# Sliding-window attention mixed with a SwiGLU FFN: the softmax division in the tail, first sums in fp32, operands on multiples of 256 bytes, the first tail tile halved early

## The chip, the cores and the metric

The kernel runs on one core of a Trainium2 chip. The metric is the device time of one execution in microseconds (us), taken as the median of several executions. PE is TensorE (matmuls; PEld its weight loads), DVE is VectorE, ACT is ScalarE, POOL is GpSimd; SP issues nearly all DMAs and POOL the others.

## The reference

With x of 2048 x 512, 32 heads of 16, a causal window of W = 256 keys and an FFN of 1792 columns, all float32:

```python
scores = jnp.einsum("bhqd,bhkd->bhqk", q, k) * (Dh ** -0.5)
mask = (idx[:, None] - idx[None, :] >= 0) & (idx[:, None] - idx[None, :] < W)
p = _softmax(jnp.where(mask[None, None], scores, -1e9), axis=-1)
a = (p @ v, heads joined) @ wo                    # in short
b = (_silu(x @ w_gate) * (x @ w_up)) @ w_down
g = _sigmoid((x * gate_w).sum(-1, keepdims=True))
return g * a + (1 - g) * b
```

## The kernel before, in words

**Number format.** TensorE takes fp32r operands. To keep float32 precision, each operand is split into hi (a cast to fp32r) and lo (the rest), and every product is three matmuls: hi by hi, hi by lo, lo by hi. `split` makes the two; `mm3` issues the three. A cast runs on ACT or DVE, the subtraction on DVE or POOL. The program is a manual schedule: each engine runs its instructions in the order in which the code issues them, and waits by semaphores.

**Start (0 to 87 us).** Twelve-odd DMAs bring x (transposed, `xT`), the q/k weights and `wv`. `split_x` makes `xhi`/`xlo`, four chunks of 512 positions, that stay for the whole program. Eleven small products of `ident` warm TensorE. `proj(g, c)` makes q and k of group g (four heads) for chunk c, by `whole`: a PSUM bank of 128x512 and 12 matmuls. `vproj` makes v. `stack` copies the parts of q and k by DMA into `QT` and `KT`, 63 rows deep, so that one matmul gives a score with all three partial products; row 63 holds the maximum of the row (`QT`) and ones (`KT`). `stage1` makes scores of a block of 128 queries, and DVE adds the mask and takes the row's maximum; `put_max` transposes the maxima on PE by `ident`, negates them and loads row 63. `prefetch` fetches the next tile of FFN or q/k weights and `prepare` splits it on ACT (hi) and POOL (lo).

**Slots (87 to 611 us).** 129 slots, 16 for each of 8 groups. A slot has `stage1` of the next group, `stage2` of this one (transposed scores, exponent on ACT, masks on POOL), and a quarter of a unit of `lanes`: two 512-column sums at once, each product done as two matmuls of 64 rows that run beside each other. The units are the q/k sums of later groups and 26 of the 28 sums of the FFN's gate and up tiles; these go to DRAM (`raws`). Every fourth slot `av` multiplies probabilities by v (`vg`, with a column of ones that gives the softmax's sum), and `finish` adds the two half sums, transposes on DVE, takes the reciprocal, multiplies, transposes back and writes to `od` by a DMA of POOL. In the last group the gate is made (`gate_fetch`, `gate_block`), and eight tiles of w_down are split (`wd_early`).

**Tail (611 to 842 us).** 4 chunks c of 14 FFN tiles n. `hidden` loads the two sums of a tile (`got`), takes silu on ACT and the product on DVE; `halved` splits that into `hh` (ACT) and `hl` (DVE); `step(c, n)` is 12 matmuls that add this tile's part of the output for four blocks into four PSUM banks. Tile 13's sums are the two that the slots don't make: 24 matmuls in `hidden` itself. `ORDER` sets that tile as the second. `load_wd`, `load_wo` bring weights in chunk 0. `load_oc` loads attention's output from `od`, `attn_split` splits it (ACT, POOL), `attn_out` multiplies by wo. `put` adds the terms and writes the output. SP issues the loads in the code's order and each waits for its buffer, so a load behind a waiting one waits too.

Of the kernel before, what the change touches and what calls it, by code (L numbers as in the profile page):

```python
# [16 lines left out]
P = 128  # L17
# [16 lines left out]
def gated_mix(ctx, tc, xT, xn, wqk, wv, wo, wgu, wd, gw, out):  # L34
# [22 lines left out]
    gate = const.tile([P, NB], F32, name="gate")  # L57
    igate = const.tile([P, NB], F32, name="igate")
# [82 lines left out]
    ORDER = [0, NF - 1, *range(1, NF - 1)]  # L141
# [25 lines left out]
    with ExitStack() as A:  # L167
# [4 lines left out]
        for _ in range(11):  # L172
            nc.tensor.matmul(warm[:, :P], ident, ident, start=True, stop=True)

        mask = sm.tile([P, 3 * P], F32, name="mask", bufs=1)
        nc.gpsimd.memset(mask, 0.0)
        nc.gpsimd.affine_select(out=mask, in_=mask, pattern=[[-1, 3 * P]], compare_op=ALU.is_ge,
                                fill=NEG, base=W, channel_multiplier=1)
        nc.gpsimd.affine_select(out=mask, in_=mask, pattern=[[1, 3 * P]], compare_op=ALU.is_ge,
                                fill=NEG, base=-1, channel_multiplier=-1)  # L180
# [52 lines left out]
        def proj(g, c, pool, name):  # L233
# [9 lines left out]
            return whole(pool, name, products(("p", g), c), done)  # L243
# [10 lines left out]

# [21 lines left out]
        def put_max(g, hf):  # L276
            n = NB // 2
            mt = sm.tile([4 * n, P], F32R, name="mt")
            for o in HALVES:
                pt = ps1.tile([P, CH], F32, name="ps1")  # L280
                nc.tensor.matmul(pt[:4 * n, :64], MX[g, hf].rearrange("p h b -> p (h b)")[o], ident[o, o],
                                 start=True, stop=True)
                nc.vector.tensor_scalar(mt[:, o], pt[:4 * n, :64], -1.0, None, op0=ALU.mult)  # L283
            for pr in range(2):
                nc.sync.dma_start(halves_of(QT[g % 2][pr])[hf][63::64].bitcast(F32),
                                  mt[2 * pr * n:2 * (pr + 1) * n].bitcast(F32))
# [48 lines left out]
        def finish(g, c):  # L335


# [6 lines left out]
            if lo:  # L344
                nc.vector.tensor_copy(both[:, :lo], first[:, :lo])
            yield
            ot = osb.tile([P, CH], F32, name="ot")
            nc.vector.transpose(ot, both)
            yield
            v = ot.rearrange("p (s e) -> p s e", e=32)  # L350
            rc = osb.tile([P, CH // 32], F32, name="rc")
            nc.vector.reciprocal(rc, v[:, :, DH])
            nc.vector.tensor_tensor(out=v[:, :, :DH], in0=v[:, :, :DH],
                                    in1=rc[:, :, None].to_broadcast([P, CH // 32, DH]), op=ALU.mult)
            yield
            on = osb.tile([P, CH], F32, name="on")
            nc.vector.transpose(on, ot)
            nc.gpsimd.dma_start(od[g, :, c * CH:(c + 1) * CH], on)
# [8 lines left out]
        split_wq = weights(("p", 0))  # L367
# [14 lines left out]
        def v_products(b):  # L382
            c, o = divmod(b * P, CH)
            return [(xt[c][:, k, o:o + P], wt[:, k]) for k in range(NK)
                    for xt, wt in ((xhi, wvh), (xhi, wvl), (xlo, wvh))]
# [20 lines left out]
        xraw = [halves_of(h) for h in xraw]  # L406

        def split_x(c):
            for k in range(NK):
                split(xhi[c][:, k], xlo[c][:, k], xraw[2 * c + k // 2][k % 2], nc.scalar, nc.vector)  # L410

        for c in range(NCH):
            for k in range(NK):
                nc.sync.dma_start(xraw[2 * c + k // 2][k % 2], xT[c][:, k])
            if c == 0:
                split_next = weights(("p", 1), kept(), nc.vector)
                wvraw = [fetch(wv[:, k], kept()) for k in range(NK)]
        split_wq()
# [328 lines left out]
```

## Time and profile before

| what | value |
|---|---|
| runs | 842.01, 842.23, 843.0 us; median 842.23 |
| the profiled execution, its span | 842.1 us, granted TensorE clock 0.996 on average |
| PE busy | 826.0 us, 98% |
| DVE, ACT, POOL busy | 520.7, 448.4, 351.6 us |
| moved by DMA | 133.02 MB, mean 158 GB/s |
| waits of PE that the profile names | 3.9 us on hh at the tail's start, 2.6 on ACT's copy in `finish`, 1.5 on ACT's copy of v, 1.4 on `ident`, each other 0.6 or less |

The span runs from the first instruction to the last. A row of the profile reads: line, engine, operation, written tile <- read tiles, shape, count, then busy time and mean; in a timeline the start and the length come first, and brackets hold the idle time ahead and what ended it. PE's matmuls overlap (each is shown some 390 ns long and the next starts some 230 ns later), so their pace is read from start to start.

### The profile page before, as it was taken

What the parts mean: (1) busy time and instruction counts of PE and PEld (TensorE: products, weight loads), DVE (VectorE), ACT (ScalarE), POOL (GpSimd) and SP (SyncE); (2) the same over time, 40 slices, a digit from 0 to 9 for tenths busy, and PEclk for the clock granted to TensorE, in tenths of its full rate; (3) what the DMA queues carried; (4) which work ended last, traced back from release to release, by engine and by line L of the source; (5) the groups of instructions that cost most, each with busy time, mean ns of one, the idle gap of its engine ahead of it and who ended that gap; (6) DMA issues with size and microseconds to landing.
All of it is one profiled execution on the core that took longest, in us unless ns stands there. A gap on an engine that the chain in (4) does not pass through costs nothing. (4 is left out here: it accounts for less than half of the span.)

```text
span 842.1 us, 21678 instructions
## 1 busy us (share of the span) xinstructions
PE 826.0 (98%) x8390; PEld 709.7 (84%) x8390; DVE 520.7 (62%) x1438; ACT 448.4 (53%) x933; POOL 351.6 (42%) x638
## 2 busy tenths in 40 slices
PE   8999999999999999999999999999979999999998
PEld 6787899899888888988888889889858888888886
DVE  6396577667767676676677677655567353353443
ACT  5412666666656666666656666566545433243251
POOL 7702455546546555545554654456501121011020
PEclk9999999999999999999999999999989999999999
DMA  7574525624533543542552463466679544293451
GB/s 274 160 210 146 148 80 150 193 93 135 153 135 120 158 152 110 161 156 99 153 178 95 125 186 128 134 198 211 209 250 295 172 162 163 76 298 89 150 163 51
DMA packets 66007, 133.02 MB, mean 158 GB/s; under 512 B 9456, under 2 KB 14192, under 8 KB 65904
## 3 DMA queue, kind: packets, MB, share of 16 engines
q1 hardware_dynamic: 61936, 117.74, 44.7%
q0 software_dynamic: 3968, 13.90, 4.5%
q8 instruction: 66, 1.08, 0.5%
q14 instruction: 37, 0.30, 0.1%
HBM read 60.82 MB, written 45.35 MB: 126 GB/s over the span
## 5 line engine op out<-in xcount | busy, mean ns | idle before, releaser
L269 DVE CUSTOM_DVE_ANT_0 ps<-ps,mask 128x384 f32<-128x384 f32 (+2 forms) x512 | 272.1, 540 | 143.4 <-PE ps L267 67.1
L308 ACT ACTIVATE pt<-ps 128x384 f32<-128x384 f32 (+2 forms) x512 | 241.6, 478 | 117.2 <-PE ps L267 60.2
L310 POOL TENSOR_SCALAR_AFFINE_SELECT pt<-pt 128x256 f32<-128x256 f32 x256 | 108.3, 423 | 229.2 <-ACT pt L308 225.4
L306 PE MATMUL ps<-q,k 64*128 64x384 f32 (+2 forms) x512 | 163.8, 329 | 2.6 <-ACT on L341 2.6
L267 PE MATMUL ps<-k,q 63*128 63x384 f32 (+2 forms) x512 | 163.7, 329 | 0.3 <-DVE mt L283 0.3
L218 PE MATMUL pb<-xhi,wh 64*128 64x512 f32 x512 | 118.2, 393 | 0.0
L218 PE MATMUL pa<-xhi,wh 64*128 64x512 f32 x512 | 117.1, 395 | 0.1
L218 PE MATMUL pb<-xlo,wh 64*128 64x512 f32 x512 | 117.2, 390 | 0.0
L218 PE MATMUL pb<-xhi,wl 64*128 64x512 f32 x512 | 117.1, 389 | 0.0
L218 PE MATMUL pa<-xhi,wl 64*128 64x512 f32 x512 | 115.0, 391 | 0.0
L218 PE MATMUL pa<-xlo,wh 64*128 64x512 f32 x512 | 114.7, 390 | 0.0
L267 PEld LDWEIGHTS ps<-k,q 63*128 63x128 f32 x512 | 92.8, 184 | 11.2 <-issue 5.4
L306 PEld LDWEIGHTS ps<-q,k 64*128 64x128 f32 x512 | 93.6, 184 | 9.5 <-ACT on L341 4.4
L313 POOL TENSOR_SCALAR_AFFINE_SELECT pt<-pt 128x256 f32<-128x256 f32 x224 | 97.8, 437 | 0.0
L654 DVE TENSOR_TENSOR sg<-got,sg 128x512 f32<-128x512 f32 x52 | 44.0, 846 | 64.5 <-ACT sg L653 54.6
L330 PE MATMUL ps<-pt,vg 64*32 64x320 f32 (+4 forms) x1408 | 76.0, 346 | 0.0
L330 PE MATMUL pb<-pt,vg 64*32 64x320 f32 (+3 forms) x1360 | 74.9, 350 | 0.0
L269 DVE DVE_READ_ACCUMULATOR2_ANT mx<- 128x1 f32 x512 | 71.8, 140 | 0.0
L218 PEld LDWEIGHTS pb<-xhi,wh 64*128 64x128 f32 x512 | 64.2, 185 | 4.0
L218 PEld LDWEIGHTS pb<-xhi,wl 64*128 64x128 f32 x512 | 64.4, 184 | 3.4
L330 PEld LDWEIGHTS pb<-pt,vg 64*32 64x32 f32 x1360 | 48.9, 106 | 21.1 <-ACT pt L308 5.1
L218 PEld LDWEIGHTS pa<-xhi,wl 64*128 64x128 f32 x512 | 62.0, 184 | 4.7
(143 smaller groups left out, 1661.7 us busy)
## 6 DMA issues: line engine op xcount, KB each, us to landing
raws<-ev SPq DMA_DIRECT2D x104, 256.0 KB
got<-raws SPq DMA_DIRECT2D x104, 256.0 KB
od<-on POOLq DMA_DIRECT2D x32, 256.0 KB, 2.4
q<-xhi SPq DMA_DIRECT2D x56, 128.0 KB
k<-xhi SPq DMA_DIRECT2D x56, 128.0 KB
raw<-wgu SPq DMA_DIRECT2D x28, 256.0 KB
vd<-vs POOLq DMA_DIRECT2D x8, 672.0 KB, 5.0
vg<-vd SPq DMA_DIRECT2D x32, 168.0 KB
```

The costliest lines, as they stand in the source:

```text
L218: mm = nc.tensor.matmul(ps[me], w[r], x[r], start=not second and i == 0, stop=bool(second) and i == n - 1)
L267: nc.tensor.matmul(ps[:, :n], QT[g % 2][pr][r, q0:q0 + P], KT[g % 2][pr][r, k0:k0 + n], start=True, stop=True)
L269: mx = nc.vector.tensor_tensor_reduce(out=ps[:, :n], in0=ps[:, :n], in1=mask[:, 3 * P - n:], scale=1.0, scalar=NEG, op0=ALU.add, op1=ALU.m ...
L306: nc.tensor.matmul(ps[:, :n], KT[g % 2][pr][r, k0:k0 + P], QT[g % 2][pr][r, k0:k0 + n], start=True, stop=True)
L308: BEHIND.append(nc.scalar.activation(pt[:, j, :n], ps[:, :n], AF.Exp, scale=SCALE))
L310: nc.gpsimd.affine_select(out=pt[:, :, :P], in_=pt[:, :, :P], pattern=[[0, 2], [1, P]], compare_op=ALU.is_ge, fill=0.0, base=0, channel_mu ...
L313: nc.gpsimd.affine_select(out=pt[:, :, 2 * P:], in_=pt[:, :, 2 * P:], pattern=[[0, 2], [-1, P]], compare_op=ALU.is_ge, fill=0.0, base=-1, ...
L330: nc.tensor.matmul(AV[g, c][h][32 * j:32 * j + 32, q0 - c * CH:q1 - c * CH], VG[4 * g + kb // 4][o, kb % 4, 17 * j:17 * j + 32], PT[g, kb, ...
L654: nc.vector.tensor_tensor(out=sg, in0=gu[1], in1=sg, op=ALU.mult)
```

## The change

- Softmax's division leaves `finish`. The slots write undivided sums to `od`; in the tail `load_sums` loads the softmax sums, `invert` takes one reciprocal of 128x512 on DVE and writes it to `rd`; `load_oc` loads a piece of `od` and a broadcast piece of `rd`, POOL multiplies and writes the result back into place by a DMA of its own.
- The first q/k sums (chunk 0 of groups 0 and 1) are made from raw x and raw weights in float32, 4 products each in place of 12; the splits of these weights, the mask and the fills come behind. The warm-up is 6 products.
- `put_max` transposes on DVE and goes by DRAM (`mxd`); `get_max` loads row 63 a slot later; `KT`'s row 63 is -1.
- `gate` and `igate` (64 bytes a partition each) are allocated ahead of `xhi`/`xlo`.
- In the start, `prefetch` is issued ahead of the stacks, and banks pa and pb change roles in `vproj2` and the last `proj`.
- Tile 0 of chunk 0 is made and halved in slots 113 to 120 (silu by exp, add, reciprocal, two products); tile 13 is third in `ORDER`; six w_down tiles are early, eight in the tail; the gate is made four slots earlier.
- The last two steps are interleaved by block, each followed by its `put`.

```diff
+    gate = const.tile([P, NB], F32, name="gate")
+    igate = const.tile([P, NB], F32, name="igate")
     xhi, xlo = [], []
...
-    ORDER = [0, NF - 1, *range(1, NF - 1)]
+    MADE = 2
+    ORDER = [0, 1, NF - 1, *range(2, NF - 1)]
...
-        for _ in range(11):
+        for _ in range(6):
             nc.tensor.matmul(warm[:, :P], ident, ident, start=True, stop=True)
...
         def put_max(g, hf):
-            n = NB // 2
-            mt = sm.tile([4 * n, P], F32R, name="mt")
-            for o in HALVES:
-                pt = ps1.tile([P, CH], F32, name="ps1")
-                nc.tensor.matmul(pt[:4 * n, :64], MX[g, hf].rearrange("p h b -> p (h b)")[o], ident[o, o],
-                                 start=True, stop=True)
-                nc.vector.tensor_scalar(mt[:, o], pt[:4 * n, :64], -1.0, None, op0=ALU.mult)
+            mt = sm.tile([P, 32], F32, name="mt")
+            nc.vector.transpose(mt, MX[g, hf].rearrange("p h b -> p (h b)"))
+            u = 2 * g + hf
+            nc.sync.dma_start(mxd[u], mt)
...
         def finish(g, c):
...
-            ot = osb.tile([P, CH], F32, name="ot")
-            nc.vector.transpose(ot, both)
...
-            nc.vector.reciprocal(rc, v[:, :, DH])
...
-            nc.vector.transpose(on, ot)
-            nc.gpsimd.dma_start(od[g, :, c * CH:(c + 1) * CH], on)
+            nc.gpsimd.dma_start(od[g, :, c * CH:(c + 1) * CH], both)
...
+        def first_sums(g, w):
+            run(proj(g, 0, pp, "pa", [(w[:, k], xraw[0][k]) for k in range(NK)]))
...
         split_x(0)
-        split_next()
+        first_sums(0, wq0)
         for k in range(NK):
-            split(wvh[:, k], wvl[:, k], wvraw[k], *(dve if k % 2 else act))
-        for g in range(2):
-            run(proj(g, 0, pp, "pa"))
+            split(wvh[:, k], wvl[:, k], wvraw[k], nc.scalar, nc.gpsimd if k % 2 else nc.vector)
+        first_sums(1, wq1)
+        fill_rows(KT[0], -1.0, 0, nc.gpsimd)
+        make_mask()
+        split_w(0, wq0, nc.gpsimd)
+        split_w(1, wq1, nc.vector)
+        prefetch()
         split_x(1)
...
-            (a0, a1), (b0, b1) = vproj2(b, pp, "pa"), vproj2(b + 2, pp, "pb")
+            (a0, a1), (b0, b1) = vproj2(b, pp, "pb"), vproj2(b + 2, pp, "pa")
...
-        prefetch()
...
+        def first_tile():
+            e = kept()
+            nc.scalar.activation(e, g0, AF.Exp, scale=-1.0)
+            yield
+            nc.vector.tensor_scalar(e, e, 1.0, None, op0=ALU.add)
+            yield
+            nc.vector.reciprocal(e, e)
+            yield
+            nc.gpsimd.tensor_tensor(out=e, in0=g0, in1=e, op=ALU.mult)
...
+            split(hh0, hl0, e, nc.scalar, nc.vector)
...
+        def load_sums():
+            l = rp.tile([P, CH], F32, name="raw2")
+            nc.sync.dma_start(l, od.rearrange("g (j e) (q s) -> (g j) e q s", e=32, q=NCH)[:, DH])
+            return l
+
+        def invert(l):
+            nc.vector.reciprocal(l, l)
+            nc.sync.dma_start(rd.rearrange("h (q s) -> (h q) s", q=NCH), l)
...
         def load_oc(c, k):
...
-            nc.sync.dma_start(OC[c][:, k], heads[:, :DH, c * CH:(c + 1) * CH])
+            s = slice(c * CH, (c + 1) * CH)
+            nc.sync.dma_start(OC[c][:, k], heads[:, :DH, s])
+            nc.sync.dma_start(RC[c][:, k], rd[8 * k:8 * k + 8, None, s].to_broadcast([8, DH, CH]))
+
+            def divide():
+                o = bp.tile([P, CH], F32, name="o")
+                nc.gpsimd.tensor_tensor(out=o, in0=OC[c][:, k], in1=RC[c][:, k], op=ALU.mult)
+                nc.gpsimd.dma_start(OC[c][:, k], o)
+            return divide
...
+        def last_steps(two):
+            for b in range(4):
+                for t in two:
+                    block(b, *t)
+                put(two[0][0], b, ACC[two[0][0]][b], igate)
+
+        seq = [(c, n) for c in range(NCH) for n in range(NF)][1:]
+        loads = [(c, ORDER[n]) for c, n in seq if n != MADE]
...
+        fresh, waiting, ready = [], [(0, 0, hh0, hl0)], []
+        sums = load_sums()
         for c, n in seq:
...
-            if c == 0 and n < NF - 8:
-                ready.append(load_wd(ORDER[n + 8], pieces[n + 8], raw2()))
+            if c == 0 and n == 1:
+                ready.append(lambda: invert(sums))
+            if c == 0 and n + 5 < NF:
+                ready.append(load_wd(ORDER[n + 5], pieces[n + 5], raw2()))
...
             if c == 0 and n >= NF - 4:
-                load_oc(0, n - NF + 4)
-            if c and 1 <= n < 5:
-                load_oc(c, n - 1)
+                ready.append(load_oc(0, n - NF + 4))
+            if c and MADE < n < MADE + 5:
+                ready.append(load_oc(c, n - MADE - 1))
```

Three places show how the order changes. On SP in the start, where the first FFN weights (`raw<-wgu`) stand among the transfers of `stack` (`q<-x..`, `k<-x..`). Before:

```order
L251 DMA k_351<-x10lo 32x1024
L250 DMA q_349<-x10lo 32x1024
L251 DMA k_351<-x10hi 32x1024
L72 DMA raw<-wgu 128x512 x2
L285 DMA q_85<-mt 2x8x128
L285 DMA q_86<-mt 2x8x128
```

After:

```order
L416 DMA q_126<-xT 128x512 x4
L416 DMA k_127<-xT 128x512 x4
L416 DMA k_128<-xT 128x512 x4
L74 DMA raw<-wgu 128x512
L248 DMA q_87<-xhi 32x1024
L249 DMA k_89<-xhi 32x1024
```

The first weight load stood behind all 36 of the stacks' transfers and now stands ahead of the first of them.

On DVE at the tail's start: `sg` is silu times up, `hl` the low half of it, `q` and `k` the places of the w_down tiles, `raw` a buffer of 128x512 and `pb` the bank of tile 13. Before:

```order
L654 TENSOR_TENSOR sg<-got_10745,sg 128x512
L67 TENSOR_TENSOR hl<-sg,hh 128x512
L654 TENSOR_TENSOR sg<-pb,sg 128x512
L66 CAST q_348<-raw_10755 128x512
L67 TENSOR_TENSOR q_348<-raw_10755,q_348 128x512
L654 TENSOR_TENSOR sg<-got_10749,sg 128x512
L66 CAST q_348<-raw_10768 128x512
L67 TENSOR_TENSOR q_348<-raw_10768,q_348 128x512
L67 TENSOR_TENSOR hl<-sg,hh 128x512
```

After:

```order
L715 TENSOR_TENSOR sg<-got_10475,sg 128x512
L69 TENSOR_TENSOR hl<-sg,hh 128x512
L715 TENSOR_TENSOR sg<-pb,sg 128x512
L650 RECIPROCAL raw_10485<-raw_10485 128x512
L68 CAST q_331<-raw_10487 128x512
L69 TENSOR_TENSOR q_331<-raw_10487,q_331 128x512
L715 TENSOR_TENSOR sg<-got_10479,sg 128x512
L68 CAST q_331<-raw_10516 128x512
L69 TENSOR_TENSOR q_331<-raw_10516,q_331 128x512
L69 TENSOR_TENSOR hl<-sg,hh 128x512
```

The rows are those of tile 0 before and of tile 1 after, as the first tile; the reciprocal of the sums stands between tile 13's product and its `hl`, the last row.

On POOL in the tail: `wol` and `ol` are low halves of wo and of attention's output, `o` the divided output. Before, these five rows are all from the last of wo on:

```order
L67 TENSOR_TENSOR wol<-raw_11067,woh 128x512
L67 TENSOR_TENSOR ol<-xhi_69,oh 128x512 x4
L67 TENSOR_TENSOR ol<-xlo_70,oh 128x512 x4
L67 TENSOR_TENSOR ol<-xhi_71,oh 128x512 x4
L67 TENSOR_TENSOR ol<-xlo_72,oh 128x512 x4
```

After, from chunk 1's `ol` on (chunk 2's head follows):

```order
L69 TENSOR_TENSOR ol<-xlo_74,oh 128x512 x4
L662 TENSOR_TENSOR o<-xhi_75,xlo_76 128x512
L663 DMA xhi_75<-o 128x512
L662 TENSOR_TENSOR o<-xhi_75,xlo_76 128x512
L663 DMA xhi_75<-o 128x512
L662 TENSOR_TENSOR o<-xhi_75,xlo_76 128x512
L663 DMA xhi_75<-o 128x512
L662 TENSOR_TENSOR o<-xhi_75,xlo_76 128x512
L663 DMA xhi_75<-o 128x512
L69 TENSOR_TENSOR ol<-xhi_75,oh 128x512 x4
```

Between one chunk's `ol` and the next's stand four products and four DMAs of POOL's own, each behind its product.

More of the change, by code (lines that the diff above doesn't have):

```diff
@@ L384, in v_products @@
             return [(xt[c][:, k, o:o + P], wt[:, k]) for k in range(NK)
-                    for xt, wt in ((xhi, wvh), (xhi, wvl), (xlo, wvh))]
+                    for xt, wt in ((xhi, wvh), (xlo, wvh))] + \
+                   [(xhi[c][:, k, o:o + P], wvl[:, k]) for k in range(NK)]
         def put_v(b, ps):
@@ L527, in wd_early, with first_load, gate_done @@
             later(t, 2, lambda: later(t + 1, 2, load_wd(f, piece, kept())))
-        pieces = [h for two in (QT[0], KT[0], QT[1], KT[1]) for t in two for h in halves_of(t)]
-        later(g7, 1, gate_place)
-        for m in range(NB // 2):
-            for b in (2 * m, 2 * m + 1):
-                later(g7 + 2 * m, 1, lambda b=b: gate_fetch(b))
-                later(g7 + 2 * m + 1, 3 * (b % 2), lambda b=b: gate_block(b))
-            wd_early(g7 + 2 * m, ORDER[m], pieces[m])
+        pieces = [h for t in (*QT[0], KT[0][0], *QT[1], KT[1][0], KT[0][1]) for h in halves_of(t)]
+        GATE0 = g7 - 4
+        later(GATE0 - 1, 1, gate_place)
+        for b in range(NB):
+            later(GATE0 + b - 1, 3, lambda b=b: gate_fetch(b))
+            later(GATE0 + b, 3, lambda b=b: gate_block(b))
+        for m in range(6):
+            wd_early(g7 + 2 * m, ORDER[m], pieces[m])
+        hh0, hl0, g0, u0 = (KT[0][1][:, i * CH:(i + 1) * CH] for i in range(4))
+        g0, u0 = g0.bitcast(F32), u0.bitcast(F32)
+        def first_tile():
[7 more added lines that the diff above has]
+            nc.gpsimd.tensor_tensor(out=e, in0=g0, in1=e, op=ALU.mult)
+            yield
+            nc.gpsimd.tensor_tensor(out=e, in0=e, in1=u0, op=ALU.mult)
+            yield
+            split(hh0, hl0, e, nc.scalar, nc.vector)
+            yield
+        FT = first_tile()
+        def first_load():
+            nc.sync.dma_start(g0, raws[0, 0, 0])
+            nc.sync.dma_start(u0, raws[0, 1, 0])
+        later(g7 + 1, 2, first_load)
+        for m in range(6):
+            later(g7 + 3 + m, 2, lambda: run(FT, 1))
+        def gate_done():
+            nc.scalar.activation(gate, gate, AF.Exp, scale=-1.0)
+            nc.vector.tensor_scalar(gate, gate, 1.0, None, op0=ALU.add)
+            nc.vector.reciprocal(gate, gate)
+            nc.vector.tensor_scalar(igate, gate, -1.0, 1.0, op0=ALU.mult, op1=ALU.add)
+        later(GATE0 + NB, 3, gate_done)
         FIN, tops = iter(()), [(0, 1)]
@@ L559, in gated_mix @@
                     while tops:
-                        put_max(*tops.pop())
+                        top = tops.pop()
+                        put_max(*top)
+                        later(t + 1, 1, lambda top=top: get_max(*top))
                     if t:
@@ L664, in gated_mix, with block, step @@
         GA = by_k(slot("k11", F32))
-        def step(c, n, hh, hl):
+        def block(b, c, n, hh, hl):
+            s = slice(b * P, (b + 1) * P)
+            mm3(ACC[c][b], [((hh[:, s], hl[:, s]), WD[ORDER[n]])], start=n == 0, stop=n == NF - 1)
+        def step(c, n, *halves):
             if n == 0:
@@ L670, in step @@
             for b in range(4):
[L671 to L672 removed]
+                block(b, c, n, *halves)
             if n == NF - 1:
```

93 lines of the change are left out of this document (46 added, 47 removed).

## The prediction

> **What bounds the kernel now.** I read the page's busy shares first, then the stretches, then the chain, then start-to-start times on TensorE, because the first view already names the engine.
>
> ```profile
> PE 826.0 (98%) x8390; PEld 709.7 (84%) x8390; DVE 520.7 (62%) x1438; ACT 448.4 (53%) x933; POOL 351.6 (42%) x638
> ```
>
> Busy time in five stretches (start, first scores, slots, first chunk of the tail, rest); granted clock, DMA share and GB/s are the last columns:
>
> ```profile
> 0.00:38.00 38.00, 35.20 (x151) 27.58 (x153) 19.54 (x23) 21.76 (x37) 28.16 (x38) 1.00 0.71 227
> 38.00:87.00 49.00, 47.40 (x391) 39.48 (x387) 35.44 (x134) 9.97 (x19) 12.30 (x12) 1.00 0.56 163
> 87.00:611.00 524.00, 521.08 (x6896) 461.33 (x6893) 358.85 (x1134) 328.93 (x725) 282.09 (x568) 1.00 0.47 147
> 611.00:658.00 47.00, 42.23 (x172) 33.13 (x170) 29.84 (x47) 22.30 (x38) 7.30 (x6) 0.93 0.83 270
> 658.00:842.00 184.00, 180.09 (x791) 148.19 (x790) 77.01 (x102) 65.45 (x115) 21.71 (x16) 1.00 0.44 144
> ```
>
> PE is the first column after the length. It idles 2.9 of 524 us in the slots, so there only PE's own pace counts; idle time to win lies in the first 87 us (4.4) and in 611 to 658 (4.8, plus a clock of 0.93). What DVE, ACT or POOL save elsewhere is worth nothing directly.
>
> PE's own pace differs by operand. The chain's last stretch, 57 tail matmuls from the first row's start to the second's:
>
> ```profile
> 822.95 0.23 PE pb L84
> ...
> 835.87 0.24 PE ps L84
> 836.13 2.79 DVE k L623 x4
> ```
>
> 12.92/57 = 226.7 ns for a 128x512 matmul. The same shape with xhi/xlo (47 starts between the first two rows), and pairs of half-row matmuls of the slots (23 pairs and three L306 pairs between the third and the last):
>
> ```profile
> 25.21 0.39 PE L198 MATMUL pa<-xhi,wh 128*128 128x512 f32 x1
> ...
> 36.13 0.39 PE L198 MATMUL pa<-xhi,wl 128*128 128x512 f32 x1
> ...
> 570.40 0.55 PE L218 MATMUL pa<-xhi,wh 64*128 64x512 f32 x2
> ...
> 571.80 0.48 PE L306 MATMUL ps<-q,k 64*128 64x384 f32 x2
> 571.98 0.54 PE L218 MATMUL pa<-xhi,wh 64*128 64x512 f32 x2
> ...
> 576.26 0.55 PE L218 MATMUL pb<-xhi,wl 64*128 64x512 f32 x2
> ```
>
> 10.92/47 = 232.3 ns; (5.86 - 3 x 0.18)/23 = 231.3 ns. In the built program wh, wl, wd, hh, hl begin on multiples of 256 bytes, xhi and xlo 128 bytes past one. Every matmul at 231 to 232 has one of these two as an operand, and none at 227 has.
>
> **The change, part by part.**
>
> Alignment. `gate` and `igate` (64 bytes each) now stand ahead of xhi/xlo, which then begin on multiples of 256. How many matmuls that touches:
>
> ```profile
> 87.00:611.00 524.00, 436.59 (x3063) 318.73 (x3060) 1.00 0.47 147
> ```
>
> With the 295 ahead of 87 us that is 3358 half-row records of L218, nominally 1680 pairs: 1680 x 4.6 = 7.7 us. The full-row ones are 120 that remain at L198 and 96 in the tail: 216 x 5.6 = 1.2 us. Together -8.9; ends 0 (the address is not the cause) and -8.9. I take -8.9, since the split by operand has no exception. [...]
>
> Start. First sums are made in fp32 from raw x and raw weights: 16 records in place of 24.
>
> ```profile
> 1.43 4.73 PE L173 MATMUL pa<-ident 128*128 128x128 f32 x22 [1.43 <-POOL ident masks.py:199]
> 5.92 0.47 PE L198 MATMUL pa<-xhi,wh 128*128 128x512 f32 x1
> ...
> 7.76 0.49 PE L198 MATMUL pa<-xhi,wh 128*128 128x512 f32 x1 [0.63 <-ACT xhi L64]
> ...
> 13.77 0.39 PE L198 MATMUL pb<-wvh,xhi 128*128 128x512 f32 x1
> ```
>
> An fp32 product is two records here: 22 of 128 columns take 4.73 us, 215 ns each, at the clock before it is released. Eight products of 512 columns are 16 x 0.86 = 13.8 us at that pace and 6.9 at twice it, against 7.85 between 5.92 and 13.77. The split of x no longer stands ahead of them, but x still has to land. I take 0.3 us gained (ends -2 and +3, a clock released late because only six warm-up products are left).
>
> Three waits on PE go:
>
> ```profile
> 36.45 0.49 PE L218 MATMUL pa<-wvh,xhi 64*128 64x512 f32 x1
> 37.19 0.49 PE L218 MATMUL pa<-wvh,xhi 64*128 64x512 f32 x1 [0.25 <-ACT ev L241]
> ...
> 62.93 0.40 PE L218 MATMUL pb<-wvh,xlo 64*128 64x512 f32 x1
> 64.78 0.98 PE L218 MATMUL pa<-wvh,xhi 64*128 64x512 f32 x2 [1.46 <-ACT vs L389]
> ```
>
> The lanes now begin in bank pb, not the pa that ACT is still copying: 0.74 - 0.23 = 0.5. At 64.78 ACT was behind its cast of the first wgu piece, whose load stood behind the stack transfers on SP; `prefetch()` is now ahead of them: 1.85 - 0.23 = 1.6. The last `proj` gets the free bank: about 0.3, worked out as half the first. The price: masks and fills move later on POOL, ahead of the first scores; if they are late, up to 1 us returns. Start in all -2.7 (ends -4.4, all the idle time there is, and +3).
>
> put_max. Its PE transposes and their PSUM wait go; a DVE transpose, one write and four row loads on SP come, used five slots later at the earliest.
>
> ```profile
> L281 PE MATMUL ps<-ident,mx 64*32 64x64 f32 x64 | 5.1, 228 | 0.0
> ```
>
> This is no complete row of idle time, only of busy time, in which pairs overlap; ends 0 and -5.1. I take -2.0: 32 pairs at 0.06, which is what is left of 0.23 where the pair overlaps its neighbours. SP's extra rows stand where it waits anyway.
>
> finish. DVE loses two transposes, a reciprocal and a multiply per finish. PE waited for none of them, so 0; a second `on` buffer frees ACT's copy from the earlier od write, also 0, as PE waits later.
>
> Tail start. Before:
>
> ```profile
> 617.37 0.40 PE L650 MATMUL pb<-xhi,wl 128*128 128x512 f32 x1
> 621.67 0.79 PE L82 MATMUL ps<-q,hh 128*128 128x512 f32 x1 [3.91 <-ACT hh L64]
> ...
> 622.69 0.63 PE L84 MATMUL ps<-q,hl 128*128 128x512 f32 x1
> 623.12 0.63 PE L82 MATMUL ps<-q,hh 128*128 128x512 f32 x1
> ...
> 627.18 0.39 PE L83 MATMUL ps<-q,hh 128*128 128x512 f32 x1
> 627.80 0.50 PE L84 MATMUL ps<-q,hl 128*128 128x512 f32 x1 [0.24 <-DVE hl L67]
> ```
>
> PE waits 4.1 us for the first hh, then runs 0.43 apart until about 626.9: 12 x 0.2 = 2.4 us of half clock. With the first tile halved in the slots that step can start at once, which would win about 6.5. But `invert`'s reciprocal of 128x512 now stands on DVE after the multiply of tile 13 and ahead of that tile's hl; it waits for the sums, whose load waits for the last od write. Its price, from the nearest rows:
>
> ```profile
> L352 DVE RECIPROCAL rc<-ot 128x16 f32<-128x16 f32 x32 | 8.0, 249 | 0.0
> L576 DVE TENSOR_SCALAR gate<-gate 128x16 f32<-128x16 f32 x1 | 0.1, 132 | 0.0
> ```
>
> (249 - 132)/16 = 7.3 ns an element over a plain operation: 512 are 3.7 us, with a plain 128x512 operation's 0.69 about 4.4; the low end is 0.69. I take 4.4. [...] Behind it wait two wd splits, the next multiply, then hl(13): step 2 then starts some 6 us after step 1 ends instead of at once, and so long an idle time has halved the clock here, as above. So 6.5 won and 5.1 + 2.4 lost: +1.0 (ends -6.5 and +5, where wo, sums and wd collide further).
>
> Division. Per chunk and k one od load, one broadcast load of rd, a POOL multiply and a write-back must precede ACT's oh cast. For chunks 2 and 3 SP issues them later still:
>
> ```profile
> 735.93 0.33 SPq L624 DMA_DIRECT2D out<-k  x1
> ...
> 750.70 0.61 ACT L64 CAST oh<-xhi 128x512 fp32r<-128x512 f32 x1
> ...
> 751.39 1.38 POOL L67 TENSOR_TENSOR ol<-xhi,oh 128x512 fp32r<-128x512 f32 x1 [38.82 <-DMA got<-raws]
> ```
>
> ```profile
> 780.85 2.79 PE pa L650 x12
> ```
>
> ```profile
> 626.00:636.00 10.00, 9.76 (x41) 7.62 (x41) 9.62 (x18) 4.89 (x8) 0.00 (x0) 0.96 0.92 316
> ...
> 746.00:756.00 10.00, 10.00 (x46) 8.28 (x45) 6.71 (x8) 5.47 (x10) 2.90 (x2) 1.00 1.00 332
> ```
>
> ```profile
> od<-on POOLq DMA_DIRECT2D x32, 256.0 KB, 2.4
> ```
>
> PE needs oh for attn_out eight steps of 2.72 us (twelve matmuls) after 735.9, at 757.7: it was 7.0 us early. Now tile 13's hidden group falls behind that point too, 24 matmuls or 5.6 us: 12.6. The DMA engines are full there. Eight further pieces of 256 KB in a chunk are 2.1 MB, 6.3 us at 332 GB/s; loads two steps later cost up to 5.4, POOL's multiply 1.4 (as its ol) and the write 2.4: 15.5 in series, 2.9 too late, and in time where they overlap. I take a wait of 1.25 us in each of the two chunks: +2.5 (ends 0 and +6). Chunk 0's heads are loaded a dozen steps ahead of need and chunk 1's loads stand behind no out writes: 0.
>
> Last steps. They are interleaved by block, so three of the four L623 puts come ahead of the end: -0.3 of the 2.79 shown, as out writes still follow the last one.
>
> Sum on the profiled execution's 842.1: -8.9 - 2.7 - 2.0 + 1.0 + 2.5 - 0.3 = -10.4, so 831.7. The median of the runs, 842.23, is 0.1 above: **831.8**.
>
> **Rivals.** (a) *The tail's start really gains.* Reciprocal near 0.69, or the sums early enough that it lies in DVE's idle time: the tail start gives -5 in place of +1.0: 825.8; without division waits 823.3. For it: DVE's small share in the tail. Against: DVE was 9.6 of 10 us busy from 626. (b) *The address isn't the cause.* Then 8.9 comes back: 840.7, still a little faster or the same. For it: those at 227 are all of the tail, those at 231 mostly of other stages. Against: attn_out (pb at L82 to L84) is another product with other weights, lies among those 57 matmuls and is as fast. (c) *The other side: transfers of the division delay the steps themselves.* In chunks 2 and 3 at 736 to 756, DMA share 1.00, got loads stand behind od and rd loads on SP, silu and hl come late and PE waits each step. There are 34 new pieces of 256 KB in the tail, 26.9 us at 332 GB/s. The other terms sum to -12.9, so it decides at 14.6 us uncovered (843.9), over half of it: 844 and more. Against: over 658 to 842 the DMA share is 0.44.
>
> **How the numbers follow.** My forecast (827 to 837) 0.60, (a) 0.18, (b) 0.14, (c) 0.07. The range of 823 to 840 drops the lower part of (a), half of (b) and (c), about 0.2. Within 0.2% (840.5 to 843.9), about what a measurement of this kernel tells from no change, lies nearly half of (b): 0.07; slower is (c): 0.07; faster the rest.
>
> **What the profile after would show.** L218 pairs at 227 ns and a slots stretch 7 to 10 us shorter; no gap at 62.9; a DVE reciprocal of 128x512 near 4.4 us after the first od landed, and PE idle about 6 us after the second step, clock below 1; waits of PE on ACT's oh in chunks 2 and 3. I am wrong if L218 stays at 231, or if PE waits in every chunk's steps for got loads.

## The result, and the profile after

The changed kernel takes 875.32 us (median of 4 runs, 870.67 to 876.89) against 842.12 for the kernel before: a ratio of 1.038 with a 95% interval of 1.0346 to 1.0413. It is 33 us slower; the prediction was 831.8 with a range of 823 to 840, and gave "slower" a chance of 0.07. The profiled executions have spans of 873.0 and 842.1 us, and the account below is made of these.

The busy shares of the page after:

```profile
span 873.0 us, 21487 instructions
...
PE 830.6 (95%) x8308; PEld 694.0 (79%) x8308; DVE 482.9 (55%) x1294; ACT 449.3 (51%) x935; POOL 379.2 (43%) x672
```

PE is busy 4.6 us longer although it issues 82 instructions fewer, and its share fell from 98% to 95%: it now idles, and runs at half clock, which counts as busy (the mean granted clock is 0.98). Where, the transposed scores show: the same 512 matmuls (line 306 before, 305 after), with the start of the first and of the last ahead of the semicolon. Before, then after:

```profile
L306 PE MATMUL ps<-q,k x512: 217/330/442, 84.9 to 606.9; 64*128 64x384 f32 x149, 64*128 64x256 f32 x11, 64*128 64x128 f32 x11
```

```profile
L305 PE MATMUL ps<-q,k x512: 217/330/443, 85.4 to 608.2; 64*128 64x384 f32 x149, 64*128 64x256 f32 x11, 64*128 64x128 f32 x11
```

The start is 0.5 us longer (85.4 against 84.9), the slots 0.8 (522.8 against 522.0), the tail 29.6 (264.8 against 235.2). The slots' 0.8 hides two parts: up to slot 108 the changed kernel gains 5.1 us, and in the last group it gives 5.9 back.

What PE waited for, by engine, tile and line, with the total in us, the number of times and the longest (after):

```profile
PE pb L84 <- ACT oh L66: 17.0, 3, 7.7
PE ps L86 <- DVE hl L69: 6.0, 2, 5.4
PE ps L264 <- DMA k<-xhi: 3.3, 2, 2.6
PE ps L84 <- ACT hh L66: 2.8, 2, 1.6
...
PE pb L216 <- ACT ev L501: 1.5, 2, 1.0
```

The first row is new and is the tail's loss: three times attn_out stands ready and oh, the cast of the divided attention output, is not there. The chain of waits of the longest stretch but one (chunk 2) shows why; start, length, what:

```profile
748.08 8.58 DMA xlo<-rd
...
756.68 11.73 DMA xlo<-rd
...
768.58 1.26 POOL o L662
...
770.13 2.98 DMA xhi<-o
...
775.24 0.80 PE pb L86
```

Two broadcast loads of rd, 256 KB each, take 8.6 and 11.7 us, one behind the other; then come the product and its write-back, and only then the cast. The chunk's eight pieces (four of od, four of rd) take 26.6 us, from the issue of the first, at 741.80, to the landing of the last, at 768.41. PE meanwhile:

```profile
766.36 0.39 PE L86 MATMUL ps<-q,hl 128*128 128x512 f32 x1
773.88 0.79 PE L84 MATMUL pb<-woh,oh 128*128 128x512 f32 x1 [7.13 <-ACT oh L66]
...
776.26 0.63 PE L85 MATMUL pb<-wol,oh 128*128 128x512 f32 x1
776.68 0.63 PE L86 MATMUL pb<-woh,ol 128*128 128x512 f32 x1
```

It idles 7.1 us and then runs at 0.43 us from start to start instead of 0.227 (the granted clock is 0.50 from 769.0 to 779.2). Over PE's start-to-start times, everything above 0.227 us around the three waits adds up to 4.7 us in chunk 0's, 10.2 in chunk 2's and 10.6 in chunk 3's: 25.4 of the tail's 29.6.

The tail's start, where the prediction saw the reciprocal:

```profile
624.41 3.35 DVE L650 RECIPROCAL raw<-raw 128x512 f32<-128x512 f32 x1 [1.15 <-DMA raw<-od]
...
630.36 0.68 DVE L69 TENSOR_TENSOR hl<-sg,hh 128x512 fp32r<-128x512 f32 x1
```

```profile
625.34 0.39 PE L85 MATMUL ps<-q,hh 128*128 128x512 f32 x1
631.10 0.79 PE L86 MATMUL ps<-q,hl 128*128 128x512 f32 x1 [5.37 <-DVE hl L69]
631.69 0.63 PE L84 MATMUL ps<-q,hh 128*128 128x512 f32 x1
```

This is as forecast: reciprocal, two w_down splits, the next product, then hl of tile 13 at 630.4, and PE idle 5.4 us ahead of it and at half clock behind it (starts 0.43 apart until 635.9).

### The profile page after: what moved, and what is told of

Its sections match the earlier page's. It is cut to its first block, busy times and chain, and to the rows that moved or that the text cites. A ratio compares the mean times of both kernels' runs of the same rounds, so it can differ in the third digit from the quotient of the medians.

```text
span 873.0 us, 21487 instructions
## 1 busy us (share of the span) xinstructions
PE 830.6 (95%) x8308; PEld 694.0 (79%) x8308; DVE 482.9 (55%) x1294; ACT 449.3 (51%) x935; POOL 379.2 (43%) x672
## 4 chain that ended last, share of the span: by engine, by line
PE 76%; DMA 14%; POOL 3%; issue 2%; SPq 2%; DVE 2%; ACT 1%; POOLq 0%; ACTq 0%; DVEq 0%
PE pa L216 22%; PE pb L216 22%; PE pb L329 6%; PE ps L264 6%; DMA xlo<-rd 5%; PE ps L305 4%; PE ps L86 2%; PE ps L85 2%; PE ps L84 2%; DMA xhi<-rd 2%; PE pb L86 2%; PE pb L84 2%; PE pb L85 2%; PE ps L329 2%; DMA raw<-wo 1%
## 5 line engine op out<-in xcount | busy, mean ns | idle before, releaser
L309 POOL TENSOR_SCALAR_AFFINE_SELECT pt<-pt 128x256 f32<-128x256 f32 x256 | 107.8, 421 | 162.3 <-ACT pt L307 161.9
L216 PE MATMUL pb<-xhi,wh 64*128 64x512 f32 x512 | 113.0, 394 | 1.6 <-ACT ev L501 1.5
L216 PE MATMUL pa<-xhi,wh 64*128 64x512 f32 x512 | 112.3, 394 | 0.9 <-ACT ev L501 0.9
L216 PE MATMUL pb<-xlo,wh 64*128 64x512 f32 x512 | 111.5, 391 | 0.0
L216 PE MATMUL pb<-xhi,wl 64*128 64x512 f32 x512 | 111.4, 392 | 0.0
L216 PE MATMUL pa<-xlo,wh 64*128 64x512 f32 x512 | 110.5, 391 | 0.0
L216 PE MATMUL pa<-xhi,wl 64*128 64x512 f32 x512 | 110.3, 391 | 0.0
L312 POOL TENSOR_SCALAR_AFFINE_SELECT pt<-pt 128x256 f32<-128x256 f32 x224 | 93.4, 417 | 0.0
L216 PEld LDWEIGHTS pb<-xhi,wh 64*128 64x128 f32 x512 | 57.9, 185 | 9.9 <-ACT ev L501 2.2
L216 PEld LDWEIGHTS pb<-xhi,wl 64*128 64x128 f32 x512 | 57.9, 184 | 6.7
L216 PEld LDWEIGHTS pa<-xhi,wh 64*128 64x128 f32 x512 | 57.2, 185 | 7.5 <-ACT ev L501 1.6
```

What stands on the lines that cost most here:

```text
L216: mm = nc.tensor.matmul(ps[me], w[r], x[r], start=not second and i == 0, stop=bool(second) and i == n - 1)
L309: nc.gpsimd.affine_select(out=pt[:, :, :P], in_=pt[:, :, :P], pattern=[[0, 2], [1, P]], compare_op=ALU.is_ge, fill=0.0, base=0, channel_mu ...
L312: nc.gpsimd.affine_select(out=pt[:, :, 2 * P:], in_=pt[:, :, 2 * P:], pattern=[[0, 2], [-1, P]], compare_op=ALU.is_ge, fill=0.0, base=-1, ...
```

## The experiments

Each ratio below is to the kernel before, run beside that experiment.

**Is it the outermost size, the late issue, or the rd rows?** The od and rd loads have 8 heads as their outermost size. e1 changes only the order in which 8 x 16 rows lie on the 128 partitions:

```diff
-            heads = od[2 * k:2 * k + 2].rearrange("g (j e) s -> (g j) e s", e=32)
+            heads = od[2 * k:2 * k + 2].rearrange("g (j e) s -> e (g j) s", e=32)
-            nc.sync.dma_start(OC[c][:, k], heads[:, :DH, s])
-            nc.sync.dma_start(RC[c][:, k], rd[8 * k:8 * k + 8, None, s].to_broadcast([8, DH, CH]))
+            nc.sync.dma_start(OC[c][:, k], heads[:DH, :, s])
+            nc.sync.dma_start(RC[c][:, k], rd[None, 8 * k:8 * k + 8, s].to_broadcast([DH, 8, CH]))
...
-"wo": by_rows(w_o)
+"wo": by_rows(w_o.reshape(NK, 8, DH, D).transpose(0, 2, 1, 3).reshape(D, D))
```

> The changed kernel, with the rows of a head's 16 values spread in another order over the 128 partitions (and the rows of wo in the same order), so that the loads of od and rd have 16 as their outermost size instead of 8. Nothing else differs. [...] Then the rd loads get shorter than 5 us, the three waits of attn_out on oh (2.5, 7.5 and 8.1 us, with some 2.5 us of half clock behind each) shrink to under 3 us in sum, and the time falls by about 20 us, to about 855. Rival 'late issue': the chain load, load, multiply, write-back, cast stands too late behind the out writes on SP, whatever engines move it; the loads get shorter, the waits fall by less than 5 us in sum, 866 to 871. Rival 'same rows': rd is slow because 16 partitions read the same 2 KB; its loads stay over 7 us and the time stays within 3 us of 875.

Measured: 856.81 us, ratio 1.0169 (1.0135 to 1.0204), 18.5 us under the changed kernel. The waits on oh fall from 17.0 to 4.8 us, not quite to the 3 expected, and the rd load on the chain still takes 6.4 us, not under 5. The stretches with the heads' loads (columns after PEclk: DMA share, GB/s), of the changed kernel and of e1:

```profile
736.00:746.00 10.00, 10.00 (x46) 8.29 (x45) 3.69 (x6) 1.82 (x4) 0.00 (x0) 1.00 0.54 195
746.00:756.00 10.00, 10.00 (x46) 8.29 (x45) 7.16 (x10) 4.83 (x9) 2.17 (x2) 1.00 0.65 197
```

```profile
736.00:746.00 10.00, 10.00 (x46) 8.29 (x45) 5.77 (x8) 5.04 (x9) 2.19 (x2) 1.00 0.80 227
746.00:756.00 10.00, 10.00 (x46) 8.28 (x45) 4.22 (x7) 3.07 (x6) 3.75 (x4) 1.00 0.98 262
```

In these stretches 35 to 46% of the DMA engines' time went unused while loads stood in line; with 16 outermost rows it is 2 to 20%. The whole of chunk 2's eight pieces, in the changed kernel, then in e1, where the last of them had landed by 758.5:

```profile
741.80:768.41 26.61, 24.95 (x111) 20.31 (x109) 10.05 (x14) 8.21 (x14) 5.97 (x6) 1.00 0.75 232
```

```profile
742.18:758.50 16.32, 16.32 (x74) 13.51 (x73) 7.64 (x11) 5.24 (x9) 6.46 (x6) 1.00 0.94 260
```

So 26.6 us at a share of 0.75 became at most 16.3 at 0.94. (The changed kernel's share is higher towards the end, 0.85 during the last rd load, when got loads run beside it.) The order of the rows decides most of it, and the time falls nearly to the 855 expected; "same rows" is refuted, and "late issue" has at most a share: 4.8 us of wait are left. Why 16 outermost rows move faster than 8 is not shown: the profile has the mean share of all 16 engines, not the share of each.

**Does more time ahead do as well?** e6 leaves the loads as they are and issues those of chunks 2 and 3 one chunk ahead:

```diff
-            if c and MADE < n < MADE + 5:
+            if c == 1 and MADE < n < MADE + 5:
                 ready.append(load_oc(c, n - MADE - 1))
+            if 0 < c < NCH - 1 and 9 <= n < 13:
+                ready.append(load_oc(c + 1, n - 9))
```

> The changed kernel, with the loads, products and write-backs of chunks 2 and 3 issued one chunk ahead (steps 9 to 12 of the chunk before) instead of at steps 3 to 6 of their own. The loads are the same, of 8 outermost rows. Theory: the division's chain is slow but needs only time; ten steps more (27 us) hide it, and the waits of 7.5 and 8.1 us with their half clock go, 21 us, to about 854; chunk 0's wait of 2.5 us stays. [...]

Measured: 855.92 us, 1.0155 (1.0115 to 1.0196). One wait on oh is left, of 3.2 us, in chunk 0. So the chain is slow, but ten steps hide it, and the loads of 8 rows don't delay the steps there (all waits on hh and on hl come to 2.8 and 4.9 us, in the changed kernel to 2.8 and 6.0).

**Is the division all of it?** e3 puts it back into finish (the lines that the diff removed) and takes the sums, rd, products and write-backs out of the tail.

```diff
-            nc.gpsimd.dma_start(od[g, :, c * CH:(c + 1) * CH], both)
+            nc.vector.transpose(ot, both)
...
+            nc.vector.reciprocal(rc, v[:, :, DH])
...
+            nc.gpsimd.dma_start(od[g, :, c * CH:(c + 1) * CH], on)
...
-            nc.sync.dma_start(RC[c][:, k], rd[8 * k:8 * k + 8, None, s].to_broadcast([8, DH, CH]))
...
-        sums = load_sums()
...
-            if c == 0 and n == 1:
-                ready.append(lambda: invert(sums))
```

> The changed kernel, with the division back in finish as it was (two transposes, reciprocal and multiply on DVE, od written divided); no sums, no rd, no multiplies and write-backs in the tail. Theory: the division in the tail costs all of the waits on oh (18 us), the half clock behind them (7.5 us) and the reciprocal at the tail's start (about 6 us), and the slots don't notice the 70 us of DVE that come back: about 845, tail's length about 235 us as before. Rival: DVE in the slots becomes a bound in the last group, where it also splits w_down and makes the gate: the slots get over 3 us longer, 850 or more. Second rival: the waits in the tail come from the new order of got and w_down loads, not from the division: still over 860.

Measured: 846.24 us, 1.0043 (1.0024 to 1.0063). 29 us of the loss are the division's place, as the changed kernel builds it. The tail is now 233 us (610.2 to 843.4), 2 less than before. The slots notice little: PE's wait for ACT's copy in finish (line 338) goes from 1.3 to 3.9 us, because that kernel has room for one `on` buffer only: twice in the last group the copy waits some 4 us for the buffer's write to od (4.3 and 3.7). What still makes e3 slower than before is outside the tail.

**The reciprocal.**

```diff
-            if c == 0 and n == 1:
+            if c == 0 and n == 6:
                 ready.append(lambda: invert(sums))
...
-            l = rp.tile([P, CH], F32, name="raw2")
+            l = GA[:, 0]
```

> The changed kernel, with the reciprocal of the sums issued six tiles into chunk 0 instead of two, and kept in a place of its own until then. Theory 'the reciprocal delays hl': it took 3.35 us on DVE ahead of tile 13's low half, for which PE then waited 5.4 us and ran at half clock until 635.9. Then hl of tile 13 comes at about 627, PE's wait falls under 2 us, no half clock follows, and the time falls by 5 to 7 us, to 868 to 870; the reciprocal itself delays nothing later by more than 1 us. Rival 'the w_down loads set it': the two splits ahead of hl wait for their loads anyway, the wait stays over 4 us, and the time stays within 2 us of 875.

Measured: 872.14 us, 1.0343 (1.0306 to 1.038), 3.2 under the changed kernel; between the profiled executions the tail is 4.1 shorter. The wait on hl at that place is 2.3 instead of 5.4 us. Half clock follows here too, against the expectation, but for 3.4 us instead of 6.8 (starts 0.43 apart from 625.7 to 629.2). And oh of chunk 1 comes 2.0 us too late now, with half clock behind it, where at most 1 us was expected. Right in kind, less in size than the 5 to 7 expected: 2.3 us of wait stay, as the two w_down splits and the next product still stand ahead of hl.

**The address alone**, in the kernel before:

```diff
+    gate = const.tile([P, NB], F32, name="gate")
+    igate = const.tile([P, NB], F32, name="igate")
     xhi, xlo = [], []
...
-    gate = const.tile([P, NB], F32, name="gate")
-    igate = const.tile([P, NB], F32, name="igate")
```

> The kernel before, with gate and igate allocated ahead of xhi and xlo and nothing else, so that xhi and xlo begin on multiples of 256 bytes. Theory 'full rows only': the 240 matmuls of 128 rows with xhi or xlo go from 232.3 to 226.7 ns, the pairs of 64-row matmuls stay at 231 as in the changed kernel, where they did not get faster: 1.3 us less, about 840.9. Theory of the prediction: pairs too, 8.9 us less, 833.3. Rival: the address does nothing, 842.1.

Measured: 841.64 us, 0.9982 (0.9962 to 1.0002): 1.2 us less by the medians, an interval that just touches none. Its PE rows, first and last of 48 full-row matmuls, then two places 12 pairs and two pairs of scores apart:

```profile
24.55 0.39 PE L198 MATMUL pa<-xhi,wh 128*128 128x512 f32 x1
...
35.20 0.39 PE L198 MATMUL pa<-xhi,wl 128*128 128x512 f32 x1
...
571.30 0.60 PE L218 MATMUL pa<-xlo,wh 64*128 64x512 f32 x2
...
574.42 0.61 PE L218 MATMUL pb<-xlo,wh 64*128 64x512 f32 x2
```

10.65/47 = 226.6 ns: full rows do follow the address. The half-row pairs don't: 1.56 us for six pairs and their scores, against 1.57 before (570.40 to 575.11 in the trace of before is three times that). From pair to pair the median is 231.0 ns in the kernel before, in e4 and in the changed kernel. So the 231 ns go with the half-row form and not with the address; what in that form sets them is not shown. e11 asked what full rows would do there:

```diff
-                    for lane in range(2):
-                        me = lane ^ second
-                        r = slice(64 * lane, 64 * lane + 64)
-                        w, x = todos[me][i]
-                        mm = nc.tensor.matmul(ps[me], w[r], x[r], start=not second and i == 0,
...
+                    w, x = todos[second][i]
+                    nc.tensor.matmul(ps[second], w, x, start=i == 0, stop=i == n - 1)
```

> The kernel before, with xhi and xlo on multiples of 256 bytes and the units of lanes done as matmuls of all 128 rows, first one sum, then the other, instead of pairs of 64-row matmuls. The number of columns streamed is the same. Theory: the 231 ns of the pairs come from the pairing, not from the address; 1680 matmuls of 128 rows take 226.7 ns: 7.7 us less than the address alone gives, 833 to 834. Rival: full rows cannot start while the half-row scores beside them run; each change between them costs, and the time is 840 or more.

Measured: 1035.23 us, 1.228 (1.2254 to 1.2306), the rival, though far above the 840 that it named. Three full rows stand between two changes to the half-row scores:

```profile
400.42 0.50 PE L215 MATMUL pa<-xhi,wh 128*128 128x512 f32 x1
400.75 0.40 PE L215 MATMUL pa<-xlo,wh 128*128 128x512 f32 x1
400.99 0.40 PE L215 MATMUL pa<-xhi,wl 128*128 128x512 f32 x1
401.31 0.44 PE L261 MATMUL ps<-k,q 63*128 63x384 f32 x1
...
401.68 0.50 PE L215 MATMUL pa<-xhi,wh 128*128 128x512 f32 x1
```

From 400.42 to the next such place, 401.68, is 1.26 us; with pairs (297.30 to 298.17 in the trace of before) it is 0.87. There are 512 such places, and the loss of 192 us is 0.38 for each. The gaps lie at the changes: 0.32 from the last full row to the score, 0.37 from the score (401.31) to the next full row (401.68), against 0.24 and 0.17 with pairs. The rows of the weight loads (PEld) show what is lost:

```profile
400.75 0.19 PEld L215 LDWEIGHTS pa<-xhi,wl 128*128 128x128 f32 x1
401.31 0.18 PEld L261 LDWEIGHTS ps<-k,q 63*128 63x128 f32 x1 [0.37 <-DVE rc L346]
...
401.68 0.19 PEld L215 LDWEIGHTS pa<-xhi,wh 128*128 128x128 f32 x1 [0.19 <-issue]
```

Among full rows the weights are loaded ahead: those of the matmul of 400.99 at 400.75, with the start of the one before. At a change the load starts only with its own matmul, at 401.31 and 401.68, though at 401.68 the profile names nothing to wait for. All 1024 changes of e11 are like this (2 ns ahead in the median, against 0.23 us among full rows). With pairs, in the trace of before, it starts 0.23 us ahead also where pairs and scores meet (297.77 for the score of 298.00). Why the load is not ahead at a change of form is not shown.

**The rest, mended together.** e8 keeps the division in the tail, with e1, e2 and e6, the gate's slots as before (`GATE0 = g7`), and `make_mask()` and the first fill ahead of `split_x(0)`. e9 has the division in finish, and the same gate, mask and fill.

> The changed kernel with the division kept in the tail and five things mended together: loads of 16 outermost rows, the late reciprocal, the early heads, the gate where it was before (slots 112 to 127), and the mask and the fill of ones at the very start, where GpSimd was idle from 2.8 to 11.2 us. Theory: waits on oh 0 to 1 us in sum, hl of tile 13 under 2.5, no wait on the k<-xhi transfers (3.3 us), slots 108 to 129 within 2 us of before: 836 to 840. Rival: the tail's DMA work stays the bound, waits move to got or wo: over 846.

Measured: 837.92 us, 0.9945 (0.9925 to 0.9966). No wait on oh is left. Two marks were missed: hl of tile 13 is waited for 3.0 us, not under 2.5, and the slots from 108 on are 4.5 us longer than before, not within 2.

> The changed kernel with the division back in finish, the gate where it was before, and the mask and the fill at the very start. Theory: of e3's 846.2, the wait for k<-xhi (4 us) and the last group's loss (about 4 us between slots 112 and 129) go: 838 to 839, faster than before by some 0.4%. Rival: the mask and fill at the start hold up the split of x on DVE, which shares work with GpSimd, and the first group comes later: 841 or more. If the last group's loss stays with the gate moved back, the first tile made in the slots causes it, and the time is 841 to 842.

Measured: 838.85 us, 0.995 (0.993 to 0.9969). Both times are as expected, half a percent under before, and between these two the place of the division makes no difference that shows. For e9 this is partly luck: the last group's loss, which was to go, stayed for the most part (slots 108 to 129 are 4.2 us longer than before, in e3 6.8). The wait for k<-xhi is 0.7 to 0.8 us in both, 3.1 to 4.2 in every variant of the changed kernel without the early fill. The likely reason is seen on POOL, where both v writes stood behind fills and the mask in the changed kernel, and came together, as the stacks' transfers began:

```profile
27.52 1.97 POOL L386 DMA_DIRECT2D vd<-vs  x2
```

Before, they left at 22.3 and 26.6, and in e8 at 23.3 and 25.3. SP's issues of the stacks' transfers are slower behind them in the changed kernel:

```profile
29.31 1.30 SPq L249 DMA_DIRECT2D k<-xhi  x1
30.66 1.16 SPq L248 DMA_DIRECT2D q<-xhi  x1
31.92 1.43 SPq L249 DMA_DIRECT2D k<-xlo  x1
33.39 1.31 SPq L248 DMA_DIRECT2D q<-xlo  x1
```

In e8 these four take 0.5 to 0.6 us each. No run moved the v writes alone.

**The first tile.** e8 still loses 4.6 us in slots 112 to 129, with ACT waiting for an ev buffer. e13 is e8 without the first tile in the slots; e14 is e9 without it, and with heads of 16 rows.

```diff
-        later(g7 + 1, 2, first_load)
-        for m in range(6):
-            later(g7 + 3 + m, 2, lambda: run(FT, 1))
...
-        seq = [(c, n) for c in range(NCH) for n in range(NF)][1:]
+        seq = [(c, n) for c in range(NCH) for n in range(NF)]
-        fresh, waiting, ready = [], [(0, 0, hh0, hl0)], []
+        fresh, waiting, ready = [], [], []
```

> The kernel of e8 without the first tile in the slots: tile 0 of chunk 0 is loaded, gets its silu and is halved at the tail's start as in the kernel before, and everything else of e8 stays. Theory: the first tile holds one of the five buffers into which ACT empties the units' sums (ev) for five slots; ACT waits for them (0.5 to 1.9 us each, three times between 551 and 579) and slots 112 to 129 lose 4.6 us; at the tail's start it wins less, since PE then waits for the next tile's hh and for tile 13's hl. Then slots 112 to 129 come within 1 us of before, the tail gets 1 to 3 us longer, and the time is 1.5 to 3.5 us under e8's 837.9: 834.5 to 836.5. Rival: the first tile wins what it was made for, the 4.3 us wait and 2.4 us of half clock come back at the tail's start, and the time is 840 or more. Second rival: the last group's loss comes from the rest of the new order there (six early w_down tiles, gate): slots still lose 4 us or more.

Measured: 835.02 us, 0.9901 (0.9878 to 0.9924), 2.9 under e8 by the medians and the best of all. The transposed scores of e8, then of e13:

```profile
L305 PE MATMUL ps<-q,k x512: 217/330/443, 80.3 to 601.9; 64*128 64x384 f32 x149, 64*128 64x256 f32 x11, 64*128 64x128 f32 x11
```

```profile
L305 PE MATMUL ps<-q,k x512: 216/331/443, 80.8 to 597.6; 64*128 64x384 f32 x149, 64*128 64x256 f32 x11, 64*128 64x128 f32 x11
```

The slots are 4.8 us shorter, the tail 3.9 longer (233.7 and 237.6, from spans of 835.6 and 835.2), where 1 to 3 longer was expected. So the first tile wins what the tail's start can give and loses a little more in the slots. These two executions differ by 0.4 us alone; the 2.9 are between the medians, and e13's profile is of its slowest run.

> The kernel of e9 (division in finish, gate and mask as before) without the first tile in the slots, and with the heads loaded by 16 outermost rows. What is left of the change: fp32 first sums, put_max by DVE, the address, prefetch ahead of the stacks, tile 13 as third, the interleaved last steps. Theory: the same 1.5 to 3.5 us under e9's 838.9 as e13 gains over e8: 835.5 to 837.5; if division in the slots costs PE nothing, e13 and e14 agree within 1.5 us. Rival: as for e13, 840 or more.

Measured: 840.12 us, 0.9956 (0.9938 to 0.9975), with single runs from 836.2 to 845.9. No gain over e9's 838.9: a miss. In the profiled execution, one of 845.9, PE waited 7.0 us for ACT's copy in finish, in the last group, where the one `on` buffer waits for its write to od. e13, with two, waited 1.3. So e13 and e14 don't agree within 1.5 us as expected, and in that execution, the slowest of twelve, the division in the slots was not free where its buffers are short. What a typical run of e14 loses there is not shown.

**Can both be had?** e15 is e8 with the first tile's silu in one of the two buffers of the gate's rows:

```diff
-            nc.sync.dma_start(XG[2 + b % 2], xn[b * P:(b + 1) * P])
+            nc.sync.dma_start(XG[2], xn[b * P:(b + 1) * P])
...
-            e = kept()
+            e = XG[3]
```

> The kernel of e8 with one thing changed: the first tile's silu lies in the second of the two buffers of the gate's rows, and these rows go through one buffer, so that the first tile takes none of the five ev buffers. Theory: ACT finds an ev buffer free as in e13, slots 112 to 129 lose nothing, and the tail keeps e8's length (233.7 us from the last transposed score, against e13's 237.6): 4 us under e8's 837.9 and about 1 to 2 under e13's 835.0, so 832.5 to 834.5. Rival: the gate's rows through one buffer hold up DVE, or the first tile's other work (exp on ACT, a reciprocal of 3.35 us on DVE) delays the last group by itself: slots lose over 2 us, 836 or more.

Measured: 840.54 us, 0.9976 (0.996 to 0.9991): the rival. The last transposed score starts at 603.5, 1.5 us later than e8's. PE no longer waits for ev but for DVE's sum in finish (two waits of 1.5 us): that row stands on DVE behind the gate's product, which waits for the gate's rows, now through one buffer. Behind the second wait PE runs at half clock, from 578.8 to 582.2.

**The fp32 first sums.** e16 is e15 with them made of split operands, 12 products each:

```diff
-            run(proj(g, 0, pp, "pa", [(w[:, k], xraw[0][k]) for k in range(NK)]))
+            run(proj(g, 0, pp, "pa"))
...
+        split_w(0, wq0, nc.gpsimd)
...
         split_x(0)
+        split_w(1, wq1, nc.vector)
         first_sums(0, wq0)
...
-        split_w(0, wq0, nc.gpsimd)
-        split_w(1, wq1, nc.vector)
         prefetch()
```

> The kernel of e15 with the first sums of groups 0 and 1 made from split x and split weights, 12 products each, as in the kernel before; six warm-up products and all else as in e15. Theory of the prediction: the fp32 sums gain 0.3 us: this one is 0 to 1 us slower than e15, since PE waits for the splits of x between 6 and 10.5 us but streams 5.6 us instead of 6.9. Rival: the fp32 sums are worth more, because the splits of x no longer stand ahead of the first products: over 1.5 us slower. Second rival: they cost, since PE waits for raw x all the same (1.7 us at 7.0) and its 16 records of 0.43 are longer than 24 of 0.23: faster than e15.

Measured: 843.22 us, 1.0019 (0.9999 to 1.0039), 2.7 over e15: the first rival. Its first product starts at 7.06, behind the first split of x, and the first eleven run at half clock (starts 0.43 apart until 12.45); the six warm-up products had ended at 4.4. In e15 the raw sums start at 4.15, and v's first matmul already at 12.13. (e16 also splits the q/k weights earlier on POOL and DVE, which the sums need; the two are not told apart.)

## Why the prediction was wrong, point by point

- **Division, the step that failed.** It took +2.5 (ends 0 and +6) and it was 25 us, with half clock. The order of events was right (loads, product, write-back, cast, late for chunks 2 and 3). The price was not. In chunk 2 the prediction counted 15.5 us more in series against 12.6 us of room, and took 1.25 us of wait instead of the 2.9 left, as some of it would overlap. Measured, from the last out write's issue to the first oh cast it was 14.8 us before (735.9 to 750.7) and 32.8 after (740.4 to 773.2): 18 us more, and PE waited 7.1 us in chunk 2 and 7.7 in chunk 3. The eight pieces were priced at 332 GB/s, read where the DMA share was 1.00; their 26.6 us went at 232 GB/s and a share of 0.75, other loads included, and the rd loads landed one after the other. The half clock behind a long wait, which the same text priced at 2.4 us at the tail's start, was not added here; it is some 3 us in each of the two chunks. Chunk 0, set at 0, cost 4.7.
- **Rival (c)** had the right place and sign and the wrong victim: no step of chunks 2 and 3 waited for hh or hl (the two waits on hh, 2.8 us in sum, end at 622.0 and 663.4), attn_out waited. Its threshold of 14.6 us uncovered was passed.
- **Address, mis-sized.** -8.9 taken, 1.2 measured. The 216 full rows do what was said (226.6 ns). The 1680 pairs were put down to the same cause because they have the same operands; that they also differ in form was not weighed as a rival for them alone. Rival (b) was right for 7.7 of 8.9 us.
- **Start, -2.7 taken, +0.5 measured.** The three waits went, as said (no gap over 0.4 us stands between PE's starts from 42 to 538 us). The fp32 sums gave more than 0.3: v's first matmul starts at 12.7 instead of 13.8. The moved fills and mask were said to cost up to 1 us; the wait for k<-xhi cost 3.3, likely by the v writes behind them, and PE's granted clock was 0.50 behind it, from 42.0 to 45.4 us.
- **put_max, -2.0 taken.** Between slots 0 and 16 the changed kernel gains 1.6 us, and up to 108 another 3.5. Of these, 1.6 are not put_max but two gaps of 0.7 and 0.9 in the trace of before, at 367 and 434: ACT's copy in `finish` waited 3.2 and 3.4 us there for the one `on` buffer's write to od. The prediction set the second `on` buffer at 0; it took these gaps away: e4, with one buffer, has one of 2.0 at 368, and no variant with two has one there. The remaining 3.5 us are put_max's and what else changed in the slots, not told apart.
- **Last steps, -0.3 taken.** Right: from PE's last start to the end it is 4.2 us instead of 4.4.
- **Tail start, +1.0 taken.** The mechanism came as described: 3.35 us of reciprocal (4.4 taken), 5.4 us of wait, half clock. All that PE's start-to-start times have above 0.227 between 620 and 640 is 9.5 us after, and 7.8 before from 614 to 628: +1.7.
- **Left out.** The first tile and the earlier gate cost the last group 5.9 us in the slots. The prediction looked at what the tile wins in the tail and not at what it holds in the slots (4.6 us in e8, gone in e13), nor at the gate's loads, for which PE waited 1.5 us at 540. That the tile's ev buffer alone costs the 4.6 is not shown: in e15, with the tile elsewhere, other waits took its place.

## What to carry to other kernels

Before a load is put on a path with a deadline, look at its outermost size (e1 changed nothing else): with 8 rows the eight pieces of a chunk took 26.6 us and left a quarter of the DMA time unused, with 16 rows at most 16.3 us and 6%. Price a new chain by its single pieces in series at the rate of its own transfers, add the half clock that can follow a wait (here it followed waits from 1.5 us, in e15, to 7.7, but not those of 3.0 in e8 and 3.2 in e13, so no length is shown from which it sets in), and give it a chunk of lead where it has no deadline of its own. And count what a step moved into a full stage holds there, buffers as well as engine time.

## What was not expected of the hardware

The reciprocal of 128x512 took 3.35 us on DVE, 4.9 times a plain 128x512 operation (0.69): per element, 6.5 ns. Full-row fp32r matmuls of 512 columns went at 226.7 ns with both operands on multiples of 256 bytes (226.6 in e4) and at 232.3 with one of them 128 bytes past; pairs of 64-row matmuls went at 231 either way. And on PE each change between full rows and half rows, with 384 to 512 columns on either side, cost some 0.19 us (0.38 for there and back, 512 times in e11), where the weights were not loaded ahead (by 2 ns in the median, against 0.23 us among full rows); pairs of half rows, whose weights were loaded 0.23 us ahead in the kernel before, did not pay it.
